# A token gate worked in five batches in place of seven, with its logit matmuls one step later

## The chip, the cores and the metric

One core of one Trainium2 chip. The time is the device time of one execution, in microseconds (us); the profile is of one execution of the same program, and its times count from the start of its span.

## The reference

Three layers in a row, all on 4608 tokens of width 512; the kernel must give the last one's output.

```python
q_c, k_c, v_c = (a.reshape(B, H, S // 64, 64, D) for a in (q, k, v))   # B 8, H 8, S 576, D 64
s = np.matmul(q_c, k_c.transpose(0, 1, 2, 4, 3)) / np.sqrt(D)
p = np.exp(s - s.max(-1, keepdims=True))
x = np.matmul(p / (p.sum(-1, keepdims=True) + 1e-9), v_c)              # then x as [4608, 512]

xn = x / (np.linalg.norm(x, axis=-1, keepdims=True) + 1e-6)
en = expert_emb / (np.linalg.norm(expert_emb, axis=-1, keepdims=True) + 1e-6)
logits = xn @ en.T / tau                                               # 8 experts
idx, gate = logits.argmax(1), softmax(logits).max(1)
x = gate[:, None] * (np.maximum(x @ w1[idx], 0) @ w2[idx])             # one expert a token, F = 1024

h = x @ w_in                                                           # 512 -> 2048
out = (h / (1 + np.exp(-1.702 * h))) @ w_out
```

## The kernel before

The tokens are 36 tiles of 128. The order of the instructions on every engine is the order in which the program writes them; nothing is scheduled behind it. The program has three parts: attention with the gate, the experts, the last layer.

**Attention and gate.** One loop with `n` from 0 to 38 (a step). In step `n` different tiles are at different points:

- TensorE transposes a half of the next q and k (`emit_T`, L307), makes the scores of tile n (`emit_S`, L334), transposes the softmax numerators of tile n-1 (`emit_PT`, L357), multiplies tile n-2 by v (`emit_PV`, L379) and transposes the result of tile n-5 into the layout that the gate needs (`emit_XT`, L431; its second half reads what GpSimd makes). At the end of the step it makes the logits of the same tile n-5 (`emit_L`, L454) in PSUM bank `gb`.
- VectorE takes the row maximum of the scores (`max_S`, L341) and subtracts it (L344), copies the transposed tile out of PSUM (`evac_XT`, L439), scales the result of tile n-3 and rounds it to fp16 (`emit_X`, L405, L410, L415) and divides tile n-2 by its sum (`emit_x`, L387, L389, L391). These are nine instructions a step. From tile 30 on the copy is made by ScalarE (L437); from tile 33 on VectorE makes the rounding rest itself (L420).
- ScalarE copies the transposed q and k (L312, four a step) and the transposed numerators (L364), takes the exponential (L351) and the sum of squares of tile n-3 (`emit_sq`, L399).
- GpSimd makes the rounding rest of tile n-3 (L417, L418; below a pair is called X(t), t being the tile) and issues indirect DMAs.

**The gate** works on a batch of tiles when the last tile of the batch is there: `norm` (the inverse norm of x) is queued by the last tile's `emit_X`, `gate` (argmax, softmax weight, place of each token in its expert's list) by the last tile's `emit_L`. Both are Python generators in one queue `todo`; `drip(1)`, which stands at ten places of a step, issues the next VectorE instruction of the queue's first entry. So a batch's instructions are strewn singly between those of the steps. In the middle of `gate` TensorE counts ranks (L545 to L548, also in bank `gb`); `drip` passes four places before it.

When a batch's places (`pi_all`) are there, one indirect DMA a tile writes token number and weight into a table in HBM (`place`, L494, below a scatter). Even tiles write `mtab[0]`, odd ones `mtab[1]`; a scatter waits until the scatter before it on the same table has landed. `scat()` issues one if any is due: one at the start of a step, and one after X while more than four are left (any are left, from step 30).

Once 24 tiles are gated (`NPART`) the most used expert is chosen, its weights are loaded and split into two fp16 halves (`first_split`; ScalarE L786, VectorE L791, GpSimd L788 and L789) from step 33 on, and three tiles of its tokens are looked up (`find`, L851, two gathers from the tables) and fetched (`fetch`, L858, L864). `turn` transposes a fetched tile by DMA from the SP queue (L872).

**The turn to the experts.** In steps 36 to 38 and behind the loop the first quarter products of expert tiles 0 and 1 (`mm1_part`, L888) stand between the last attention work. Behind the loop the last batch is gated, its scatters are issued, the tables for all expert tiles are worked out (`tables`), and `find(3)`, `fetch(3)`, `turn(3)` bring the first tile that needs every token's place. Then the SP queue loads the next expert's weights. After that come 36 more expert tiles and the last layer, a long run of matmuls.

Of the kernel before, what the change touches and what calls it, by code (L numbers as in the profile page):

```python
# [10 lines left out]
F16 = mybir.dt.float16  # L11
# [4 lines left out]
ALU = mybir.AluOpType  # L16
# [18 lines left out]
def kernel(  # L35
# [13 lines left out]
    nc = tc.nc  # L49
    B, H, S, D = q.shape  # L50
    NT, DM = out.shape
    NE = emb.shape[0]
# [7 lines left out]
    NTILE = NT // 128  # L60
# [15 lines left out]
    att = att_stack.enter_context(tc.tile_pool(name="att", bufs=1))  # L76
# [364 lines left out]

    batches = [(0, 8), (8, 8), (16, 4), (20, 4), (24, 4), (28, 4), (32, 4)]
    DR = [1, 1, 1]
    lg_t = {}

    def emit_L(t):
        bi = [j for j, (a, n) in enumerate(batches) if a <= t < a + n][0]
        t0, n = batches[bi]
        if t == t0:
            o = 0 if bi + 1 < len(batches) else 208  # L450
            lg_t[bi] = gb[:, o:o + 2 * n * NE].rearrange("p (a e) -> p a e", a=n)
        xT = xT_t.pop(t)
        for c in range(2 * KD):
            nc.tensor.matmul(  # L454
                lg_t[bi][:, t - t0, :], xT[:, c, :], enT[:, c % KD, :],
                start=(c == 0), stop=(c == 2 * KD - 1),
            )
# [4 lines left out]
    def small(nm, n, dt=F32, w=None, bufs=1):  # L462
        t = att.tile([128, 8] if w is None else [128, 8, w], dt, tag="g_" + nm, name="g_" + nm, bufs=bufs)
        return t[:, 0:n]
# [3 lines left out]
    def norm(bi):  # L468
        t0, n = batches[bi]
        ssc, y = ss_all[:, t0:t0 + n], rn_all[:, t0:t0 + n]  # L470
        yield from rsqrt(y, small("t", n, I32), small("a", n), ssc)
        nc.vector.tensor_tensor(out=y, in0=y, in1=ssc, op=ALU.mult)
        yield
        nc.vector.tensor_scalar(y, y, 1e-6, None, op0=ALU.add)
        yield
        nc.vector.reciprocal(out=y, in_=y)
        yield
        isx = is_all[:, t0:t0 + n]
        nc.vector.tensor_scalar(
            isx.bitcast(I32), si_all[:, t0:t0 + n], float((BIAS - X_TOP) << 23), None, op0=ALU.add  # L480
        )
        yield
        nc.vector.scalar_tensor_tensor(
            out=y, in0=y, scalar=itau[:, 0:1], in1=isx, op0=ALU.mult, op1=ALU.mult
        )
        yield

    pi_all = att.tile([128, NTILE], I32, name="pi_all")
    scats = deque()
# [10 lines left out]
    def scat():  # L500
        if scats and scats[0][0] < now[0]:
            scats.popleft()[1]()

    def gate(bi):
# [8 lines left out]
        yield  # L513
        nc.vector.tensor_tensor(
            out=l, in0=l, in1=rn_all[:, T].unsqueeze(2).to_broadcast([128, n, NE]), op=ALU.mult
        )
# [16 lines left out]
        yield  # L533
        oh = att.tile([128, 8, NE], F16, tag="g_oh", name="g_oh", bufs=2)[:, 0:n]
        nc.vector.tensor_tensor(
# [5 lines left out]
        yield "pe"  # L541
        rkf = gb[:, 128:128 + n * NE]
        rk = rkf.rearrange("p (a e) -> p a e", a=n)
# [428 lines left out]
    def end_L(t):  # L972
        emit_L(t)
        for bi, (t0, nn) in enumerate(batches):
            if t == t0 + nn - 1:
                todo.append(gate(bi))
# [14 lines left out]
    back = {LATE + 2: LATE - 2}  # L991
    back.update((t + 3, t) for t in range(LATE, NTILE))
    for n in range(NTILE + 3):
        now[0] = n
# [9 lines left out]
        for f in ev[1]:  # L1004
            f()
        turned = []
        if n - 1 in back:
# [15 lines left out]
        issue_v(v_due(n))  # L1023
        if len(scats) > (4 if n < 30 else 0):
            scat()
        on(n, exp_S)
# [3 lines left out]
        if n in back:  # L1030
            emit_XT(back[n])
        for t in sorted(turned):
            end_L(t)
        if n >= NTILE - 5 and fl_n[0] < 8:
# [474 lines left out]
```

## Time and profile before

| what | value |
|---|---|
| time, median of 3 executions | 1449.27 us (1449.14 to 1451.39) |
| time of the profiled execution | 1442.4 us |
| its span in the trace | 1440.7 us |
| attention steps 5 to 31 (first L341 of step 5 to that of step 32) | 39.03 to 193.06 us |
| last L341 (step 35) | 215.14 us |
| last scatter of the last batch | 268.50 us |
| first matmul of expert tile 3 | 283.67 us |

The span begins with the first instruction and ends with the last; the time has some 2 us around it. A step is measured from one L341 of VectorE to the next, there being one in each step up to 35.

### The profile page before, as it was taken

Reading aid. Unit: us, or ns where it says so; the run is one execution under the profiler, and the core shown is the slowest. Engines: PE = TensorE matmul, PEld = TensorE weight load, DVE = VectorE, ACT = ScalarE, POOL = GpSimd, SP = SyncE. Lnnn points to the kernel's source line nnn. Section 1 sums busy time; section 2 is a strip of 40 time slices with the busy share of each in tenths; the row PEclk is TensorE's granted clock in tenths of the full one; section 3 lists DMA queues with packets and bytes.
Section 4 is the critical chain, followed back from the end, with each engine's and each line's share of the span. In section 5 each row is a group of like instructions: output and inputs, shape, how many; then the busy total and the mean of one; then the engine's idle time right before and its main releaser. Section 6 shows DMA issues by size and latency. Waiting matters only on the chain.

```text
span 1440.7 us, 31953 instructions
## 1 busy us (share of the span) xinstructions
PE 1300.4 (90%) x12802; PEld 915.1 (64%) x12802; DVE 855.3 (59%) x1681; ACT 640.1 (44%) x1125; POOL 722.7 (50%) x648
## 2 busy tenths in 40 slices
PE   6777664778989899999989999999999999999998
PEld 4666554556656667767575766758484857566673
DVE  3888886636775667876566372808173644638160
ACT  6986753224453435543453342516152524434250
POOL 1445657535666565564156262717264553626261
PEclk8998976989999999999989999999999999999999
DMA  9887865275775556885310202011020202020000
GB/s 209 216 191 173 167 131 143 68 211 132 209 209 128 162 167 183 255 215 146 69 38 16 45 1 59 2 37 23 23 38 15 45 16 45 9 51 1 30 1 30
DMA packets 196279, 140.71 MB, mean 98 GB/s; under 512 B 129928, under 2 KB 167816, under 8 KB 196112
## 3 DMA queue, kind: packets, MB, share of 16 engines
q1 hardware_dynamic: 183184, 108.39, 32.8%
q0 software_dynamic: 12768, 30.10, 6.2%
q8 instruction: 102, 1.67, 0.5%
q14 instruction: 65, 0.53, 0.1%
q10 hardware_dynamic: 160, 0.02, 0.0%
HBM read 89.00 MB, written 29.80 MB: 82 GB/s over the span
## 4 chain that ended last, share of the span: by engine, by line
PE 50%; DMA 3%; issue 0%; DVE 0%; POOL 0%; ACT 0%; POOLq 0%; DVEq 0%; ACTq 0%
PE pb L1338 6%; PE pd L1338 6%; PE pa L1338 6%; DMA xg<-xs,mt 3%; PE pc L1338 3%; PE gb L1338 3%; PE pa L1453 2%; PE pa L1452 2%; PE pa L1451 2%; PE pd L1451 2%; PE pd L1452 2%; PE pd L1453 2%; PE pb L1452 2%; PE pb L1451 2%; PE pb L1453 2%; PE gb L1452 1%
## 5 line engine op out<-in xcount | busy, mean ns | idle before, releaser
L1338 PEld LDWEIGHTS <-wS 128*128 128x128 f16 x3024 | 297.1, 98 | 42.4 <-issue 5.2
L888 PE MATMUL ph<-xTm,w1HL 128*128 128x128 f16 x3744 | 234.7, 226 | 38.8 <-DMA xTm<-xg 8.1
L888 PEld LDWEIGHTS <-w1HL 128*128 128x128 f16 x3744 | 225.5, 101 | 55.8 <-issue 19.5
L1363 POOL TENSOR_TENSOR w2HL<-z,w1HL 128x512 f16<-128x512 f32 x144 | 217.2, 1524 | 82.8 <-ACT w1HL L1362 81.3
L921 PE MATMUL py<-w2HL,hT 128*128 128x512 f16 x936 | 208.2, 379 | 0.0
L921 PEld LDWEIGHTS <-hT 128*128 128x128 f16 x936 | 89.9, 98 | 101.5
L1458 POOL DMA_INDIRECT out_dram<-y,idc x36 | 35.4, 982 | 235.0 <-ACT y L1457 195.2
L1356 ACT ACTIVATE z<-z 128x512 f32<-128x512 f32 x144 | 88.3, 629 | 107.0 <-DVE z L1353 54.4
L955 POOL DMA_INDIRECT ys<-y,idx_y x39 | 39.1, 1002 | 146.7 <-ACT hT L895 60.1
L1359 DVE TENSOR_TENSOR z<-stgB,z 128x512 f32<-128x512 f32 x108 | 105.3, 1001 | 0.0
L851 POOL DMA_INDIRECT mt<-mtab,idx_g x78 | 88.3, 1132 | 32.9 <-issue 19.7
L1453 PEld LDWEIGHTS <-w2HL 128*128 128x128 f16 x576 | 56.4, 98 | 67.9
L1451 PEld LDWEIGHTS <-w1HL 128*128 128x128 f16 x576 | 56.4, 98 | 67.0
L1452 PEld LDWEIGHTS <-w1HL 128*128 128x128 f16 x576 | 56.4, 98 | 67.0
L1362 ACT ACTIVATE w1HL<-z 128x512 f16<-128x512 f32 x144 | 86.9, 625 | 8.4 <-DVE z L1359 8.4
L417 POOL TENSOR_TENSOR x<-x,sx_all 128x512 f32<-128x512 f32 x33 | 34.3, 1039 | 85.9 <-DVE rd L387 36.8
L896 DVE SCALAR_TENSOR_TENSOR hT<-ph,hT 128x512 f16<-128x512 f32 x78 | 51.0, 683 | 42.8 <-ACT hT L895 40.5
L1175 DVE SCALAR_TENSOR_TENSOR d_f<-raw_o,d_t 128x512 int32<-128x512 int32 x32 | 68.2, 2132 | 3.1
L895 ACT ACTIVATE hT<-ph 128x512 f16<-128x512 f32 x78 | 44.3, 590 | 53.9 <-PE ph L888 49.8
L1384 DVE TENSOR_TENSOR stgB<-stgB,pb 128x512 f32<-128x512 f32 x28 | 19.1, 684 | 81.3 <-PE pb L1338 76.1
L934 ACT ACTIVATE ysq<-py 128x512 f16<-128x512 f32 x39 | 23.1, 593 | 93.8 <-PE py L921 76.2
L1384 DVE TENSOR_TENSOR stgB<-stgB,pd 128x512 f32<-128x512 f32 x27 | 18.5, 684 | 76.4 <-PE pd L1338 76.4
(277 smaller groups left out, 2756.0 us busy)
## 6 DMA issues: line engine op xcount, KB each, us to landing
stg<-in_moe_w_dram SPq DMA_DIRECT2D x14, 1024.0 KB
stgB<-in_moe_w_dram SPq DMA_DIRECT2D x14, 1024.0 KB
vt<-in_v_dram SPq DMA_DIRECT2D x64, 144.0 KB
xs<-xr SPq DMA_DIRECT2D x36, 256.0 KB
raw_o<-in_moe_w_in_dram SPq DMA_DIRECT2D x16, 512.0 KB
raw_o<-in_moe_w_out_dram SPq DMA_DIRECT2D x16, 512.0 KB
ku<-in_k_dram SPq DMA_DIRECT2D x12, 512.0 KB
qu<-in_q_dram SPq DMA_DIRECT2D x12, 512.0 KB
```

The costliest lines, as they stand in the source:

```text
L851: nc.gpsimd.indirect_dma_start(out=mt_t[i][a][:, :], out_offset=None, in_=mtab[a][:, :], in_offset=bass.IndirectOffsetOnAxis(ap=idx_g[:, i ...
L888: nc.tensor.matmul(p[:, f % 4], wt[:, c, fs], xT[:, a, :], start=(c == 0 and a == 0 and wt is w1H), stop=(c == KD - 1 and wt is w1L),)
L921: nc.tensor.matmul(p, hT[:, a, :], wt[:, c, :], start=st, stop=sp)
L1175: nc.vector.scalar_tensor_tensor(out=fi, in0=hi, scalar=-(1 << 31), in1=t, op0=ALU.bitwise_and, op1=ALU.bitwise_or)
L1338: nc.tensor.matmul(dst, wS[a][:, o, kc, fs], rhs(b, kc), start=first and ab == 0 and kc == 0 and n == 0, stop=(kc == 1 and n == 2), skip_g ...
L1356: nc.scalar.activation(out=z, in_=z, func=AF.Sigmoid, scale=1.702 * 2.0 ** -G_EXP)
L1359: nc.vector.tensor_tensor(out=z, in0=c, in1=z, op=ALU.mult)
L1362: nc.scalar.activation(out=dst[0], in_=z, func=AF.Copy)
L1363: nc.gpsimd.tensor_tensor(out=dst[1], in0=z, in1=dst[0], op=ALU.subtract)
L1451: nc.tensor.matmul(p, gT[0][:, h, c, tt], wo[0][:, c, :], start=(c == 0), stop=False)
L1452: nc.tensor.matmul(p, gT[0][:, h, c, tt], wo[1][:, c, :], start=False, stop=False)
L1453: nc.tensor.matmul(p, gT[1][:, h, c, tt], wo[0][:, c, :], start=False, stop=(c == KG - 1))
```

## The change

The seven batches (8, 8, 4, 4, 4, 4, 4 tiles) become five (10, 10, 4, 6, 6). In `norm` the scale of the tile is folded into the addition and the temperature is taken into a multiplication of `gate`. The logits of a tile are made at the start of the step after its copy rather than at the end of the same step, up to step 34. After X up to two scatters may be issued in place of one, and from step 28 on none are held back. Columns of bank `gb` are laid out anew and tiles are made for ten.

```diff
-    batches = [(0, 8), (8, 8), (16, 4), (20, 4), (24, 4), (28, 4), (32, 4)]
+    batches = [(0, 10), (10, 10), (20, 4), (24, 6), (30, 6)]
...
-            o = 0 if bi + 1 < len(batches) else 208
+            o = 0 if bi + 1 < len(batches) else 416
...
-        nc.vector.tensor_scalar(y, y, 1e-6, None, op0=ALU.add)
+        nc.vector.scalar_tensor_tensor(
+            out=y, in0=y, scalar=1e-6, in1=sx_all[:, t0:t0 + n], op0=ALU.add, op1=ALU.mult
+        )
...
-        )
-        yield
-        nc.vector.scalar_tensor_tensor(
-            out=y, in0=y, scalar=itau[:, 0:1], in1=isx, op0=ALU.mult, op1=ALU.mult
         )
...
-        nc.vector.tensor_tensor(
-            out=l, in0=l, in1=rn_all[:, T].unsqueeze(2).to_broadcast([128, n, NE]), op=ALU.mult
+        nc.vector.scalar_tensor_tensor(
+            out=l, in0=l, scalar=itau[:, 0:1], in1=rn_all[:, T].unsqueeze(2).to_broadcast([128, n, NE]),
+            op0=ALU.mult, op1=ALU.mult,
         )
...
-        rkf = gb[:, 128:128 + n * NE]
+        rkf = gb[:, 272:272 + n * NE]
...
+        if n <= NTILE - 2:
+            for t in turned:
+                end_L(t)
         turned = []
...
-        if len(scats) > (4 if n < 30 else 0):
-            scat()
+        for _ in range(2):
+            if len(scats) > (4 if n < 28 else 0):
+                scat()
...
-        for t in sorted(turned):
-            end_L(t)
+        if n >= NTILE - 2:
+            for t in sorted(turned):
+                end_L(t)
```

How the instructions stand now is shown at three places. In the built program a batch has 33 VectorE instructions before the change and 32 after it.

TensorE between step 5 and step 6, where the eight logit matmuls (L454, two rows shown) and the transposes of the next k (L307) meet:

```order
 L379 MATMUL db<-vt_89,PT 64x65 x16
-L454 LDWEIGHTS xTa
-L454 MATMUL gb<-enT,xTa 128x16
...
 L307 MATMUL tp<-identF,ku 128x128 x8
+L454 LDWEIGHTS xTa
+L454 MATMUL gb<-enT,xTa 128x16
...
 L431 LDWEIGHTS xr
```

The logits have moved behind the transposes of q and k and stand directly ahead of `emit_XT`.

GpSimd where the first batch's table entries are scattered (L494 before, L492 now), before the change:

```order
L494 DMA mtab1_77<-meta_154,pi_all_178 36864x2
L494 DMA mtab0_76<-meta_154,pi_all_178 36864x2
L417 TENSOR_TENSOR x_1656<-x_1656,sx_all_173 128x512
L418 TENSOR_TENSOR xr_1718<-x_1656,xr_1718 128x512
```

and now (these are the scatters of tiles 1 to 6 about X(15)):

```order
L492 DMA mtab1_77<-meta_154,pi_all_178 36864x2
L492 DMA mtab0_76<-meta_154,pi_all_178 36864x2
L492 DMA mtab1_77<-meta_154,pi_all_178 36864x2
L417 TENSOR_TENSOR x_1850<-x_1850,sx_all_173 128x512
L418 TENSOR_TENSOR xr_1912<-x_1850,xr_1912 128x512
L492 DMA mtab0_76<-meta_154,pi_all_178 36864x2
L492 DMA mtab1_77<-meta_154,pi_all_178 36864x2
L492 DMA mtab0_76<-meta_154,pi_all_178 36864x2
```

Two scatters between one X and the next became three; there are three in two gaps of the first batch, in three gaps of the second, and in one of the third batch (tiles 20 to 23), behind which all six gathers of `find(0)` to `find(2)` stand in one run ahead of X(30).

VectorE around the scaling of tile 34 (L405) in step 37, before the change:

```order
L509 COPY g_dl_3932<-gb_74 128x32
L512 TENSOR_TENSOR g_l_3934<-gb_74,g_dl_3932 128x32
L514 TENSOR_TENSOR g_l_3934<-g_l_3934,rn_all_177 128x32
L519 TENSOR_REDUCE g_mx_3937<-g_l_3934 128x4
L521 TENSOR_TENSOR g_l_3934<-g_l_3934,g_mx_3937 128x32
L526 SCALAR_TENSOR_TENSOR g_w_3972<-g_l_3934,io_re_128 128x32
L532 TENSOR_REDUCE g_mw_3974<-g_w_3972 128x4
L405 TENSOR_SCALAR si_all_172<-ss_all_171 128x1
```

and now:

```order
L391 TENSOR_TENSOR x_3823<-db_170,rd_3822 128x2x4x64
L576 CAST pi_all_178<-g_pf_3828 128x6
L790 SCALAR_TENSOR_TENSOR w1HL_79<-stg1_82,w1HL_79 128x512
L405 TENSOR_SCALAR si_all_172<-ss_all_171 128x1
```

The seven instructions of the gate of tiles 28 to 31 that stood ahead of it are gone; that batch no longer exists, and the gate of tiles 24 to 29 has ended by then.

## Rows read from the trace of the kernel before

**Rows 1.** The page, first part: busy us, share, instructions of each engine.

```profile
PE 1300.4 (90%) x12802; PEld 915.1 (64%) x12802; DVE 855.3 (59%) x1681; ACT 640.1 (44%) x1125; POOL 722.7 (50%) x648
```

**Rows 2.** Timeline, expert tiles 3 and 4: start, us, work, idle before, releaser.

```profile
283.67 8.02 PE L888 MATMUL ph<-xTm,w1HL 128*128 128x128 f16 x96 [6.60 <-DVE y L951]
...
305.02 5.71 PE L888 MATMUL ph<-xTm,w1HL 128*128 128x128 f16 x62 [8.14 <-DMA xTm<-xg]
```

**Rows 3.** Windows: length, busy PE, PEld, DVE, ACT, POOL (instructions), clock, DMA.

```profile
39.03:61.55 22.52, 17.89 (x461) 15.45 (x461) 18.25 (x45) 21.70 (x42) 10.51 (x11) 1.00 0.89 216
...
39.03:161.86 122.83, 89.78 (x2051) 76.83 (x2050) 104.20 (x300) 96.56 (x184) 63.85 (x60) 0.91 0.84 191
...
161.86:229.83 67.97, 38.08 (x785) 31.57 (x783) 54.13 (x174) 37.27 (x71) 42.28 (x42) 0.75 0.65 131
```

**Rows 4.** Lines of VectorE, 39.03 to 161.86: busy, mean ns, idle before.

```profile
L341 DVE TENSOR_REDUCE mx<-sp 128x8 f32<-128x512 f32 x23 | 15.9, 689 | 15.2 <-PE sp L334 15.2
```

**Rows 5.** Timeline, step 14, the second half of a batch's gate.

```profile
86.04 0.35 PE L454 MATMUL gb<-enT,xTa 128*128 128x16 f16 x8 [2.07 <-DVE g_po L572]
...
89.75 0.69 DVE L341 TENSOR_REDUCE mx<-sp 128x8 f32<-128x512 f32 x1 [2.17 <-PE sp L334]
```

**Rows 6.** Timeline, steps 10 and 17, without gate work.

```profile
61.55 0.69 DVE L341 TENSOR_REDUCE mx<-sp 128x8 f32<-128x512 f32 x1 [0.62 <-PE sp L334]
...
65.60 1.17 POOL L418 TENSOR_TENSOR xr<-x,xr 128x512 f16<-128x512 f32 x1
...
102.27 0.61 PE L431 MATMUL sp<-ident,xr 128*128 128x128 f16 x8
...
103.57 0.69 DVE L341 TENSOR_REDUCE mx<-sp 128x8 f32<-128x512 f32 x1 [0.60 <-PE sp L334]
```

**Rows 7.** Timeline, scatters of tiles 1 and 3, and TensorE behind them.

```profile
95.12 1.01 POOL L494 DMA_INDIRECT mtab<-meta,pi_all  x1 [0.17 <-issue]
...
103.86 1.01 POOL L494 DMA_INDIRECT mtab<-meta,pi_all  x1 [4.16 <-DMA mtab<-meta,pi_all]
...
109.27 0.61 PE L431 MATMUL sp<-ident,xr 128*128 128x128 f16 x4 [2.12 <-POOL xr L418]
```

**Rows 8.** Timeline of GpSimd, scatters of tiles 9, 11 and 13.

```profile
144.02 1.01 POOL L494 DMA_INDIRECT mtab<-meta,pi_all  x1 [0.16 <-issue]
...
150.01 1.01 POOL L494 DMA_INDIRECT mtab<-meta,pi_all  x1 [0.67 <-DMA mtab<-meta,pi_all]
...
154.99 1.01 POOL L494 DMA_INDIRECT mtab<-meta,pi_all  x1 [0.39 <-DMA mtab<-meta,pi_all]
```

**Rows 9.** Timeline, the last batch's first and third scatter.

```profile
262.80 1.34 POOL L494 DMA_INDIRECT mtab<-meta,pi_all  x1 [0.82 <-DVE ttmp L647]
...
266.89 1.31 POOL L494 DMA_INDIRECT mtab<-meta,pi_all  x1 [1.49 <-DMA mtab<-meta,pi_all]
```

**Rows 10.** Timeline of GpSimd, a find, a split and a fetch.

```profile
212.21 0.98 POOL L851 DMA_INDIRECT mt<-mtab,idx_g  x1 [0.15 <-issue]
213.50 1.19 POOL L851 DMA_INDIRECT mt<-mtab,idx_g  x1 [0.30 <-issue]
214.70 1.06 POOL L788 TENSOR_TENSOR stg<-stg,w_pow 128x512 f32<-128x512 f32 x1
...
222.05 0.19 POOL L858 TENSOR_TENSOR mt<-mt,mt 128x2 int32<-128x2 int32 x1
...
223.52 1.05 POOL L788 TENSOR_TENSOR stg<-stg,w_pow 128x512 f32<-128x512 f32 x1
```

**Rows 11.** Timeline, TensorE behind X(32).

```profile
229.89 0.61 PE L431 MATMUL sp<-ident,xr 128*128 128x128 f16 x4 [5.44 <-POOL xr L418]
```

**Rows 12.** Timeline, steps 37 and 38: squares of tiles 34, 35, scaling of 34.

```profile
233.79 0.63 ACT L399 ACTIVATE sq<-x 128x512 f32<-128x512 f32 x1 [0.65 <-DVE is_all L479]
...
239.24 0.14 DVE L405 TENSOR_SCALAR si_all<-ss_all 128x1 int32<-128x1 int32 x1
...
244.75 0.62 ACT L399 ACTIVATE sq<-x 128x512 f32<-128x512 f32 x1
```

More of the change, by code (lines that the diff above doesn't have):

```diff
@@ L462, in small @@
     def small(nm, n, dt=F32, w=None, bufs=1):
-        t = att.tile([128, 8] if w is None else [128, 8, w], dt, tag="g_" + nm, name="g_" + nm, bufs=bufs)
+        t = att.tile([128, 10] if w is None else [128, 10, w], dt, tag="g_" + nm, name="g_" + nm, bufs=bufs)
         return t[:, 0:n]
@@ L533, in gate @@
         yield
-        oh = att.tile([128, 8, NE], F16, tag="g_oh", name="g_oh", bufs=2)[:, 0:n]
+        oh = att.tile([128, 10, NE], F16, tag="g_oh", name="g_oh", bufs=2)[:, 0:n]
         nc.vector.tensor_tensor(
@@ L992 @@
     back.update((t + 3, t) for t in range(LATE, NTILE))
+    turned = []
     for n in range(NTILE + 3):
```

## The prediction

> **What bounds the kernel now.** I read the page first, to see which part has room. TensorE is busy 90% of the span [rows 1]; the experts and the last layer are matmul after matmul and the change does not touch them. So it can only move the moment at which they begin. The timeline shows that moment: the matmuls of expert tile 3 start at 283.67 after 6.60 us of idle TensorE, those of tile 4 at 305.02 after 8.14, the latter for a DMA [rows 2]. By the program the way there is one chain: the last batch's gate, its scatters, `find(3)`, `fetch(3)`, `turn(3)`, and behind `turn(3)` on the SP queue the next weights, in whose traffic tile 4's transfer stands. TensorE is waiting at its end, so what the chain's start gains or loses passes to the end of the kernel in full.
>
> The chain's start is set by attention. The windows, cut where steps begin, show two kinds of step. Steps 5 to 9 hold no gate work: 22.52 us for five, 4.50 each, and ScalarE is busy 21.70 of it [rows 3]. There ScalarE is the bound, and nothing in this change makes it faster. Steps 5 to 26 together take 122.83 us; 22 steps at 4.50 would be 99.1, so the gate costs 23.7 us there. VectorE ran 300 instructions in it [rows 3]; 22 steps at nine are 198 and one more begins at the window's edge, so 101 belong to the gate: 0.235 us of lengthened step for each. That is the price of a gate instruction here, waits included.
>
> Within that price VectorE waited 15.2 us for scores [rows 4]. Of these 0.60 a step is ScalarE's limit showing [rows 6]; the rest has a place. In step 14 the logits waited 2.07 us on TensorE for the gate's product with the ranks (both use `gb`), the transposes and the scores stood behind them, and VectorE then waited 2.17 for the scores [rows 5].
>
> GpSimd is the third thing to read. Its X pair ends 5.2 us after a step's L341 (61.55 to 66.77), and TensorE wants it two steps later, for the second half of `emit_XT`, 1.0 us ahead of that step's L341 (103.57, the transposes having begun at 102.27) [rows 6]: with steps of 4.50 a pair may be 2.8 us late. A scatter waits for the one before it on its table. From one start to the other that took 8.7 us (95.12 to 103.86), and the X behind it made TensorE wait 2.12 [rows 7]; it took 6.0 and 5.0 in a quieter place [rows 8] and 4.1 in the last batch [rows 9]. I call this the landing.
>
> **The change part by part.**
>
> *Fewer gate instructions.* Two batches of 33 go and five lose one each (the order shows one, not two): 71 fewer. Up to step 26 the order has 66 where there were 101. 35 x 0.235 = **8.2 us less**. By busy time the price is nearly the same: 18.25 us of VectorE in five empty steps make 80.3 for 22, and (104.20 - 80.3) / 101 = 0.237. The least is half of that: an empty step leaves VectorE (22.52 - 18.25) / 5 = 0.85 us free, and what is removed from a step with few gate instructions falls into that gap. I take 8.2, since most gate steps hold eight to ten. The longer rows (80 columns for 64) I cost at nothing: a row's length is the small part of instructions this short, and 0.02 us on 32 would be under 1 us.
>
> *Logits behind the transposes of q and k.* TensorE no longer holds these transposes back while it waits for `gb` or for the copy. The steps that gain are those with a batch's second half. Of these two lie in the stretch after the change (16 and 26); three did before, and step 14 shows 2.17 [rows 5]. I take three quarters of it for each: **3.3 less**. It is nothing if scores still come last for another reason, and 6.5 if two thirds of all waits in gate steps (15.2 less 0.6 for each of nine steps without gate work leave 9.8, for three batches) go [rows 4]. In empty steps it gains nothing, ScalarE being full.
>
> *Three scatters between two X's.* Here the change adds a wait, and what is queued behind it on GpSimd is X, and behind X `emit_XT` and the scores on TensorE. With landing L, from the first L341 of step 17, the first batch runs so: X(14) ends at 5.2, scatters start at 5.3 and 6.6, the third at 5.3 + L. With L = 5.5, X(15) ends at 14.1 where TensorE wants it at 12.5: 1.6 late. The next three start at 14.3, 16.3 and 19.8, X(16) ends at 23.0 and is wanted at 17.0 + 1.6: 4.4 late. Together 6.0; the row of before already held 2.1 of such a wait [rows 7], so **3.9 more**. The same walk gives 3.2 in place of 6.0 for L = 4.1, and 12.4 for L = 8.7.
>
> *Steps 27 to X(32).* Before, from 161.86 to 229.83, 67.97 us [rows 3]; TensorE at its end waits 5.44 us for X(32) [rows 11], so GpSimd is the bound. It now holds 14 scatters in place of eight, but the six gathers of the finds stand in one run and do not each wait for a landing. Walked in the same way, with 1.29 for a gather, 2.2 for an X or a split, 1.47 for a fetch [rows 10] and the step lengths above, X(32) ends at 67.2: **0.8 less**. L = 4.1 gives 60.7 (7.3 less), L = 8.7 gives 86.9 (18.9 more).
>
> *Steps 37 and 38.* Tile 34's squares end at 234.4, but its scaling starts at 239.24, behind seven gate instructions; the squares of tile 35 follow at 244.75 [rows 12]. Without them the scaling can follow the split, about 4 us sooner, and TensorE's next quarter with it; VectorE's division of tile 35 and TensorE's earlier work take part of it back. I take **3.0 less**, between 0 and 4.8.
>
> *Six scatters in the last batch in place of four.* The third started 4.1 us after the first [rows 9]; another pair puts the same distance on the chain, with TensorE idle at its end: **4.1 more**. Nothing hides it. `find(3)` comes that much later, `turn(3)` on SP with it, and the weights behind that.
>
> Which L? Rows give 4.1 to 8.7. I take 5.5, between the two of rows 8, which are successive scatters amid gate work, as here; 8.7 lies in a burst of loads, 4.1 where few are left. The sum: -8.2 - 3.3 + 3.9 - 0.8 - 3.0 + 4.1 = **-7.3 us**. The profiled execution took 1442.4 and would take 1435.1; the median of the runs is 6.9 above the profiled one, and I set the sum against it: 1449.3 - 7.3 = **1442.0**.
>
> Against this stands a fixed cost. The Trainium skill, "DMA: Bandwidth & Descriptors", section "Anatomy of one DMA — SWDGE (gpsimd) path", puts a DMA issued from GpSimd at about 2.0 us plus its bytes, whatever else runs. With the 1.0 us of issue in rows 8 that would make the landing an estimated 3.0, the three scatters nearly free and the sum -23 (the first rival's). The rows, 4.1 to 8.7, differ with the traffic and decide it.
>
> **The rivals.**
>
> *Landings are short.* With fewer waits elsewhere scatters may land sooner than any row shows. At L = 3.0, 1.1 below the shortest row, the walks give 1.0 (net -1.1) for the first batch and 56.4 (-11.6) for steps 27 on: -8.2 - 3.3 - 1.1 - 11.6 - 3.0 + 4.1 = -23.1, **1426**. For it: the third scatter of rows 8 waited only 0.39. Against: every landing in the rows is longer.
>
> *GpSimd becomes the bound: slower.* At L = 8.7, +10.3 and +18.9 in place of 3.9 and -0.8: +18.8, **1468**; at 7.0, about +5, **1454**. The sign turns at 6.4. For it: the empty steps 17 to 21, where the first batch's scatters fall, move data at 216 GB/s [rows 3], as in the burst of rows 7. Against: once TensorE stalls, it frees load buffers more slowly and the traffic thins.
>
> *Nothing comes of it.* If the logits' move gives nothing, a gate instruction costs half of what I take, and the rest stands, the sum is -8.2/2 + 3.9 - 0.8 - 3.0 + 4.1 = +0.1, **1449**. That the description promises two operations a batch and the program drops one is worth 5 x 0.235 = 1.2 us and decides nothing.
>
> The transfers are not the next bound: 122.83 us at 191 GB/s are 23.5 MB, which at 216 GB/s take 109 us, 14 less than now [rows 3], more than the terms ask. TensorE's clock is 1.00 in the empty steps and 0.91 over the stretch [rows 3]; a denser TensorE may keep it up, more stalls may drop it, and I cost neither.
>
> **How the numbers follow.** What a measurement of this kernel tells from no change is about 0.2%, 2.9 us. The forecast, L between 4.1 and 6.0, has 0.45 and its own range of 1433 to 1446; short landings 0.18; landings over 6.4 have 0.22; nothing comes of it 0.15. Faster by 0.2%: nearly all of the first two and a little of the last, 0.65. Within: 0.15. Slower: 0.20. The range, 1427 to 1455, leaves out the ends of the two rivals.
>
> **What the profile of the changed kernel would show.** Between the first L341 of step 5 and that of step 27 under 117 us, with 265 VectorE instructions. In steps 16 and 26 a wait before L341 under 1 us, and L454 with hardly any. At X(15) and X(16) L431 waiting for L418, some 6 us together; if that is over 10, or the third scatters wait over 5 us, GpSimd has become the bound and I am wrong. From step 27 to the end of X(32) about 67 us. From the last batch's first scatter to its last about 10 us in place of 5.7, and tile 3's matmuls still waiting. If they no longer wait, the chain is not where I put it, and the gain of attention is not the gain of the kernel.

## The result and the profile after

The changed kernel takes 1456.8 us in the median of 22 runs, the kernel before 1449.2 in 22 runs on the same chip: a ratio of 1.0067, 95% interval 1.0049 to 1.0084. The ratio is taken over the fast executions alone, so it is not quite that of the two medians, 1.0052. The change makes the kernel slower; the forecast was 0.5% faster. The profiled execution took 1449.5 us and its span is 1447.8 us, 7.1 more than before.

The page's first part [rows 1] shows that the work did shrink: 71 VectorE instructions fewer, 12 us of VectorE less. The time did not follow it.

```profile
PE 1308.7 (90%) x12800; PEld 917.1 (63%) x12800; DVE 843.2 (58%) x1610; ACT 637.7 (44%) x1123; POOL 721.7 (50%) x648
```

The end of the chain, on the timeline [rows 2]: expert tile 3 starts at 290.46, 6.8 us later than before. From there to the end of the span it is 1157.3 us, against 1157.0. So all of the loss lies ahead of tile 3.

```profile
290.46 7.25 PE L887 MATMUL ph<-xTm,w1HL 128*128 128x128 f16 x96 [12.27 <-DMA xTm<-xg]
...
308.21 8.35 PE L887 MATMUL ph<-xTm,w1HL 128*128 128x128 f16 x96 [5.32 <-DMA xTm<-xg]
```

The windows, cut as before [rows 3]: steps 5 to 9, steps 5 to 26, and step 27 to the end of X(32) at 232.78.

```profile
38.33:59.33 21.00, 18.67 (x460) 15.33 (x459) 18.24 (x45) 20.63 (x41) 10.14 (x10) 1.00 0.94 225
38.33:158.44 120.11, 91.02 (x2070) 75.03 (x2073) 95.36 (x264) 94.09 (x181) 59.07 (x55) 0.91 0.91 197
158.44:232.78 74.34, 41.70 (x780) 33.02 (x769) 49.56 (x155) 37.75 (x73) 46.74 (x47) 0.70 0.58 121
```

From one stretch to the next: step 5 starts 0.7 us sooner; steps 5 to 26 take 120.1 in place of 122.8; step 27 to X(32) 74.3 in place of 68.0; X(32) to tile 3 57.7 in place of 53.8. Together -0.7 - 2.7 + 6.4 + 3.8 = +6.8. The empty steps take 4.20 us, not 4.50, and still the front gained only 2.7 us. The first batch's scatters show why, on the timelines of GpSimd, TensorE and VectorE [rows 7]:

```profile
98.72 1.01 POOL L492 DMA_INDIRECT mtab<-meta,pi_all  x1 [0.16 <-issue]
100.04 1.13 POOL L492 DMA_INDIRECT mtab<-meta,pi_all  x1 [0.30 <-issue]
109.15 0.97 POOL L492 DMA_INDIRECT mtab<-meta,pi_all  x1 [7.99 <-DMA mtab<-meta,pi_all]
...
111.27 1.15 POOL L418 TENSOR_TENSOR xr<-x,xr 128x512 f16<-128x512 f32 x1
```

```profile
112.48 0.61 PE L431 MATMUL sp<-ident,xr 128*128 128x128 f16 x4 [5.39 <-POOL xr L418]
...
120.59 0.61 PE L431 MATMUL sp<-ident,xr 128*128 128x128 f16 x4 [2.45 <-POOL xr L418]
```

```profile
115.47 0.69 DVE L341 TENSOR_REDUCE mx<-sp 128x8 f32<-128x512 f32 x1 [9.46 <-PE ptp L357]
```

Three scatters stand between two X's. The third shares its table with the first, whose landing took 109.15 - 98.72 = 10.4 us; X(15) stands behind it, TensorE's transposes behind X, the scores behind those, and VectorE waits 9.46 us (its row names the transposes that follow the scores on TensorE): step 19 takes 13.35 us.

The wait costs more than itself. The granted clock of TensorE is 1.00 in steps 5 to 9; from 112.48 to 116.20, behind its wait of 5.39 us, it is 0.50 (1.2 of 2.4 GHz), and the scores take 1.14 us where they took 0.69:

```profile
54.55 0.69 PE L334 MATMUL sp<-kuT,quT 64*64 64x64 f32 x32
...
113.02 1.14 PE L334 MATMUL sp<-kuT,quT 64*64 64x64 f32 x32
```

Over step 27 to X(32) the granted clock is 0.70 where it was 0.75, and nearly the same matmuls keep TensorE busy 41.70 us in place of 38.08. How much of these 3.6 us lies on the chain, no run separates.

The second batch repeats the wait for a landing behind step 27, with 171.36 - 163.91 = 7.5 us [rows 8]. Its row names a store as what ended the wait; with four tables (an experiment below) the same scatter waits 0.30 us, so it is the table it waits for:

```profile
163.91 1.01 POOL L492 DMA_INDIRECT mtab<-meta,pi_all  x1 [0.15 <-issue]
...
171.36 0.97 POOL L492 DMA_INDIRECT mtab<-meta,pi_all  x1 [5.17 <-DMA xs<-xr]
...
205.08 0.97 POOL L492 DMA_INDIRECT mtab<-meta,pi_all  x1 [5.19 <-DMA mtab<-meta,pi_all]
```

The last batch, on GpSimd [rows 9]:

```profile
264.51 1.48 POOL L788 TENSOR_TENSOR w2HL<-stg,w2HL 128x512 f16<-128x512 f32 x1
266.15 1.04 POOL L492 DMA_INDIRECT mtab<-meta,pi_all  x1 [0.16 <-issue]
...
270.20 0.97 POOL L492 DMA_INDIRECT mtab<-meta,pi_all  x1 [1.74 <-DMA mtab<-meta,pi_all]
...
276.64 0.97 POOL L492 DMA_INDIRECT mtab<-meta,pi_all  x1 [1.40 <-DMA mtab<-meta,pi_all]
```

From first to last it takes 10.5 us in place of 5.7, and the first no longer waits for VectorE (0.82 in [rows 9]) but follows GpSimd's splits at once: GpSimd is late there by itself.

### The profile page after: what moved, and what is told of

Read it like the earlier page. It is cut to its first block, busy times and chain, and to the rows that moved or that the text cites. A ratio compares the mean times of both kernels' runs of the same rounds, so it can differ in the third digit from the quotient of the medians.

```text
span 1447.8 us, 31872 instructions
## 1 busy us (share of the span) xinstructions
PE 1308.7 (90%) x12800; PEld 917.1 (63%) x12800; DVE 843.2 (58%) x1610; ACT 637.7 (44%) x1123; POOL 721.7 (50%) x648
## 4 chain that ended last, share of the span: by engine, by line
PE 49%; DMA 3%; issue 1%; POOL 0%; ACT 0%; POOLq 0%; DVE 0%; DVEq 0%; ACTq 0%
PE pb L1343 6%; PE pd L1343 6%; PE pa L1343 6%; DMA xg<-xs,mt 3%; PE pc L1343 3%; PE gb L1343 3%; PE pa L1458 2%; PE pa L1457 2%; PE pa L1456 2%; PE pd L1458 2%; PE pd L1456 2%; PE pd L1457 2%; PE pb L1458 2%; PE pb L1456 2%; PE pb L1457 2%; PE gb L1458 1%
## 5 line engine op out<-in xcount | busy, mean ns | idle before, releaser
L1361 ACT ACTIVATE z<-z 128x512 f32<-128x512 f32 x144 | 88.3, 629 | 107.5 <-DVE z L1358 54.7
L1458 PEld LDWEIGHTS <-w2HL 128*128 128x128 f16 x576 | 56.3, 98 | 68.0
L1457 PEld LDWEIGHTS <-w1HL 128*128 128x128 f16 x576 | 56.3, 98 | 67.1
L1456 PEld LDWEIGHTS <-w1HL 128*128 128x128 f16 x576 | 56.3, 98 | 67.0
L1367 ACT ACTIVATE w1HL<-z 128x512 f16<-128x512 f32 x144 | 86.9, 624 | 8.4 <-DVE z L1364 8.4
```

The costliest lines, as they stand in the source:

```text
L1361: nc.scalar.activation(out=z, in_=z, func=AF.Sigmoid, scale=1.702 * 2.0 ** -G_EXP)
L1367: nc.scalar.activation(out=dst[0], in_=z, func=AF.Copy)
L1456: nc.tensor.matmul(p, gT[0][:, h, c, tt], wo[0][:, c, :], start=(c == 0), stop=False)
L1457: nc.tensor.matmul(p, gT[0][:, h, c, tt], wo[1][:, c, :], start=False, stop=False)
L1458: nc.tensor.matmul(p, gT[1][:, h, c, tt], wo[0][:, c, :], start=False, stop=(c == KG - 1))
```

## The experiments

Each kernel was timed in turn with the kernel before on one chip; a ratio is to that kernel. Chips differ (the kernel before takes 1434.7 to 1435.1 us in the first twelve runs' medians, 1445.4 in the last two), so ratios are compared and not times. The stretches of a kernel come from one profiled execution; the executions of one kernel on one chip lie 3 to 24 us apart, so a difference of a us or two between two kernels' stretches is a hint and no proof. The theories: **S**, three scatters between X's wait for landings; **T**, the last batch of six is the loss; **D**, the steps wait for loads; later **N**, the second batch of ten puts its scatters behind step 27, and **Q**, X being late holds the SP queue (the store of x waits in it for X), whose loads then come late. The stretches below are read from the timelines in the same way as above: first L341 of step 5 to that of step 27; from there to the end of X(32); from there to tile 3.

| kernel (batches; scatters after X) | ratio, 95% interval | steps 5 to 26, us | to X(32), us | to tile 3, us |
|---|---|---|---|---|
| before (8,8,4,4,4,4,4; one) | 1 | 122.8 | 68.0 | 53.8 |
| changed (10,10,4,6,6; two) | 1.0067 (1.0049 to 1.0084) | 120.1 | 74.3 | 57.7 |
| changed, one scatter to step 27 | 1.0059 (1.0035 to 1.0082) | 120.5 | 78.0 | 56.3 |
| changed, 10,10,4,4,4,4 | 1.0068 (1.0048 to 1.0088) | 120.8 | 73.7 | 54.4 |
| before, logits moved | 0.9967 (0.9950 to 0.9984) | 117.3 | 65.5 | 56.0 |
| before, two scatters | 1.0052 (1.0032 to 1.0071) | 130.5 | 63.3 | 54.7 |
| changed, four tables | 1.0166 (1.0144 to 1.0188) | 113.4 | 71.3 | 56.2 |
| changed, store later | 1.0008 (0.9997 to 1.0019) | 118.9 | 70.8 | 57.8 |
| changed, 8,8,4,4,6,6; one | 0.9977 (0.9960 to 0.9994) | 117.7 | 64.4 | 55.0 |
| changed, 10,10,4,4,4,4; one to 27 | 1.0074 (1.0056 to 1.0092) | 117.7 | 80.1 | 54.4 |
| 8,8,4,4,6,6; one; store later | 0.9931 (0.9910 to 0.9952) | 112.3 | 62.5 | 55.6 |
| before, store later | 0.9982 (0.9967 to 0.9997) | 121.5 | 64.8 | 54.7 |
| 10,6,4,4,6,6; one | 0.9960 (0.9942 to 0.9978) | 118.9 | 64.6 | 55.4 |
| 8,8,4,4,6,6; two | 1.0052 (1.0033 to 1.0070) | 123.2 | 66.9 | 58.2 |
| 10,6,4,4,6,6; one; store later | 0.9889 (0.9859 to 0.9918) | 115.3 | 61.4 | 54.0 |
| 10,10,4,6,6; one to 27; store later | 0.9979 (0.9950 to 1.0007) | 112.0 | 75.0 | 58.5 |

### One scatter after X

```diff
-        for _ in range(2):
-            if len(scats) > (4 if n < 28 else 0):
+        for _ in range(1 if n < 28 else 2):
+            if len(scats) > (4 if n < 30 else 0):
                 scat()
```

> The changed kernel, but up to step 27 only one scatter may follow X as before the change (four are held back to step 29); two from step 28 on. Theory S (three scatters between two X's wait on GpSimd for landings of 7 to 10 us, and X, the transposes of x and the scores stand behind them): the 9.5 us of idle time in step 19 go, steps 5 to 26 fall from 120.1 us to 108 to 113, and the kernel from 1457 to 1445 to 1450. Rival T (the last batch of six decides the end): steps 5 to 26 get shorter too, but the last batch's scatters still take 10 us on the chain and tile 3 comes at about its 290 us or a little sooner; 1453 to 1457. Rival D (the steps now wait for loads, the DMA share is 0.97 in steps 5 to 16 where it was 0.83): the wait moves from the scatters to q, k, v loads, steps 5 to 26 take 117 us or more and the time stays at 1456.

Steps 19 to 21 fall from 27.5 us to 23.5, but steps 23 and 24 grow (TensorE waits 3.8 us for k there), and the stretch behind step 27 grows to 78.0. Theory S in this form falls: with batches of ten, taking the third scatter out of the gaps gains nothing. The wait moved, as D said it would: up to step 26 TensorE waits 3.2 us for X in place of 9.1, and 12.2 us for loads of k and v in place of 3.4. The last run below, which differs from this one by the store alone, shows why the loads were late.

### The old tail

```diff
-    batches = [(0, 10), (10, 10), (20, 4), (24, 6), (30, 6)]
+    batches = [(0, 10), (10, 10), (20, 4), (24, 4), (28, 4), (32, 4)]
```

> The changed kernel with the old batches at the end (10, 10, 4, 4, 4, 4 tiles), so that the last batch has four tiles again and the gate of tiles 28 to 31 is back ahead of the scaling of tile 34. Theory S: steps 5 to 26 stay at 120 us, the idle time in step 19 stays, and of the 6.8 us by which tile 3 came later only the tail's part (4.8 us between first and last scatter, 3.3 us in the queue ahead of them) can go, less the 3 us that the seven gate instructions take back: 1450 to 1454. Rival T: the tail is the whole loss, and with the old tail the earlier end of step 26 (3.4 us) shows as a gain: 1444 to 1448. Rival D says nothing of the tail: 1456.

The tail returns to 54.4 us and tile 3 starts at 287.81 in the profiled execution, 2.7 us sooner, but over all executions the ratio stays at 1.0068. T falls: the last batch of six is not what makes the kernel slower.

### The logits alone, in the kernel before

```diff
+        if n <= NTILE - 2:
+            for t in turned:
+                end_L(t)
         turned = []
...
-        for t in sorted(turned):
-            end_L(t)
+        if n >= NTILE - 2:
+            for t in sorted(turned):
+                end_L(t)
```

> The kernel before with the logits move alone: the logits of a tile stand at the start of the next step, behind the transposes of q and k, up to step 34. By the recorded prediction this gains 3.3 us in steps with a batch's second half and nothing in empty steps: steps 5 to 9 stay at 4.50 us each; 1446. By the trace of the changed kernel (its empty steps took 4.20) an empty step gains 0.3 us, and with some 13 such steps before step 27 the stretch from 5 to 27 falls by 5 to 8 us from 122.8, the kernel to 1442 to 1445. Rival D: the loads hold the steps, and the time stays at 1449.

Faster by 0.33%, 4.7 us. Empty steps take 4.20. The prediction had them at 4.50 because ScalarE was busy 21.70 of 22.52 us. The timeline shows what the other 0.8 us was: before the change, from step 8 on, ScalarE waits some 0.20 us behind the exponential (L351) for the transposes of k or q, which TensorE holds back behind the logits, and loses the overlap with the next instruction too. Kernel before, ScalarE and TensorE:

```profile
59.19 0.62 ACT L351 ACTIVATE P<-P 128x512 f32<-128x512 f32 x1
60.01 1.29 ACT L312 ACTIVATE kuT<-tp 64x512 f32<-64x512 f32 x2 [0.20 <-PE tp L307]
...
59.11 0.36 PE L454 MATMUL gb<-enT,xTa 128*128 128x16 f16 x8 [0.93 <-DVE si_all L405]
```

The changed kernel at the same place:

```profile
53.79 0.62 ACT L351 ACTIVATE P<-P 128x512 f32<-128x512 f32 x1
54.31 1.28 ACT L312 ACTIVATE quT<-tp 64x512 f32<-64x512 f32 x2
...
53.81 0.35 PE L454 MATMUL gb<-enT,xTa 128*128 128x16 f16 x8
```

0.82 us from start to start has become 0.52: that is the 0.30 of each step. What set the 4.50 was a ring of two other engines: L341, the copy (L439), the logits that wait 0.93 us for VectorE, the transposes, the scores and the next L341. In steps 5 and 6 of the kernel before, ScalarE does not wait (0.52 from start to start) and the steps take 4.51 all the same; ScalarE's wait is that ring reaching it. With the logits moved the ring is open, their row shows no wait, and 4.20 is ScalarE's own pace (busy 20.63 of 21.00 us). An engine busy 96% of a stretch was not yet the bound.

### The two scatters alone, in the kernel before

```diff
-        if len(scats) > (4 if n < 30 else 0):
-            scat()
+        for _ in range(2):
+            if len(scats) > (4 if n < 28 else 0):
+                scat()
```

> The kernel before with the scatter loop alone: up to two scatters after X, none held back from step 28 on; batches of 8, 8, 4, 4, 4, 4, 4 as before. Theory S: the wait of X behind a third scatter is there without any other part of the change, GpSimd's third scatters wait 4 to 8 us in the first two batches, TensorE's wait for the rounding rest of x grows from 11.8 us to over 16 us, and the kernel takes 1453 to 1459. Rivals T and D: the loop costs nothing by itself, 1448 to 1451. The recorded prediction's walk with a landing of 5.5 us gives 1 to 4 us more, 1450 to 1453.

Slower by 0.52%, 7.5 us. Steps 5 to 26 take 7.7 us more; the third scatters of the first two batches wait 6.12 and 4.97 us (both rows name a load of v as what ended the wait; that it is the table, the next run speaks for). TensorE's wait for X grows from 11.8 us to 15.8, just under what was expected; SP's wait for X grows from 38.2 to 45.1 us up to step 26. With batches of eight, S holds.

### Four tables

```diff
-    mtab = [dr.tile([NE * NT, 2], F32, name=f"mtab{a}") for a in range(2)]
+    mtab = [dr.tile([NE * NT, 2], F32, name=f"mtab{a}") for a in range(4)]
...
-            out=mtab[t % 2][:, :],
+            out=mtab[t % 4][:, :],
```

(`find` gathers from four tables and `fetch` adds the four.)

> The changed kernel with four tables in place of two: a scatter shares its table with the fourth before it, so three in a row never wait for one another; each find has four gathers (two more, 1.3 us each on GpSimd) and each fetch two more additions. Theory S (landing waits on GpSimd): the waits of scatters for a landing, 35.8 us between 40 and 330 in the changed kernel, fall under 12; X(15) is no longer 8 us late, step 19 falls from 13.35 us to under 7; the six more gathers of the first three finds take back 7 to 8 us ahead of X(30); 0.998 to 1.003 of the kernel before. Rival D (the loads hold the steps anyway): the scatters' waits go, the steps stay long behind q, k and v loads, 1.005 or more. A third outcome, that a scatter waits for the one before it on the queue and not on its table, would leave the 35.8 us where they are.

The waits of scatters for landings between 40 and 330 fall from 35.8 us to 7.8, step 19 to 7.03, steps 5 to 26 to 113.4: it is the table that a scatter waits for, not the queue. Behind step 27 GpSimd is busy 54.67 us in place of 46.74 for the gathers added, and the stretch takes 3.0 less all the same. Tile 3 starts at 281.98, 8.5 us sooner than in the changed kernel. That the ratio is still far over what S expected comes from behind tile 3, in the experts: from 330 to 600 the gathers keep GpSimd busy 206.5 us in place of 164.5, and TensorE is busy 235.3 in place of 247.6.

### The store of x one step later on SP

```diff
-        nc.sync.dma_start(out=xs[t * 128:(t + 1) * 128, :], in_=xrf)
+        def store():
+            nc.sync.dma_start(out=xs[t * 128:(t + 1) * 128, :], in_=xrf)
+        if t < 30:
+            late.append(store)
+        else:
+            store()
...
+        held, late[:] = list(late), []
         on(n - 3, end_X)
...
         issue_v(v_due(n))
+        for f in held:
+            f()
```

> The changed kernel with the store of a tile's x to HBM one step later in the SP queue, up to tile 29, so that the loads of v, k and q no longer stand behind a store that waits for X. Theory Q (late X holds the SP queue, the loads behind it are issued late, and TensorE later waits for k): SP's wait for X, 25.6 us between 100 and 160, falls under 5, TensorE's waits for ku go, step 27 starts 3 to 6 us sooner and the kernel is 0.2 to 0.5% faster than the changed one: 1.002 to 1.005 of the kernel before. Theory S alone: SP's wait goes too, but X(15) and X(16) are as late as they were and thicker traffic makes the landings longer: 1.006 to 1.010. Rival D: 1.006, no change.

1.0008 where the changed kernel has 1.0067: 0.6%, more than was expected. TensorE's waits for k and v loads in steps 5 to 35 are gone (6.1 us in the changed kernel); SP still waits 18.2 us for X between 95 and 160, not under 5, but with its loads ahead of it. X's own waits stay: step 19 takes 12.35.

### Front and tail apart

```diff
-    batches = [(0, 10), (10, 10), (20, 4), (24, 6), (30, 6)]
+    batches = [(0, 8), (8, 8), (16, 4), (20, 4), (24, 6), (30, 6)]
...
-        for _ in range(2):
-            if len(scats) > (4 if n < 28 else 0):
-                scat()
+        if len(scats) > (4 if n < 30 else 0):
+            scat()
```

> The changed kernel with its front batches and its scatter loop undone: 8, 8, 4, 4, 6, 6 tiles and one scatter after X. Against the kernel with the logits move alone (0.9967 of before) it has one gate operation fewer in each batch and the merged tail. Theory N (batches of ten push the second batch's scatters into the stretch behind step 27, where GpSimd is the bound): steps 5 to 26 take 115 to 118 us, X(32) ends near 222, and only the tail of six costs 2 to 6 us: 0.997 to 1.001. By the recorded terms (3.0 less in steps 37 and 38, 4.1 more in the last batch) 0.9975. Rival T (the tail is the whole loss): 1.002 to 1.005.

0.9977, by its interval not to be told from the logits alone (0.9967): merged tail and shorter `norm` together show no gain. The other half has the batches 10, 10, 4, 4, 4, 4 and the scatter loop of the first experiment:

> The changed kernel with batches of 10, 10, 4, 4, 4, 4 and one scatter after X up to step 27, two from step 28: the front's batches of ten without the three scatters in a gap and without the last batch of six. Theory N: 14 scatters still lie between step 27 and X(32), that stretch takes 73 to 78 us as in the three other kernels with batches of ten, 1.003 to 1.006. Theory S in its first form (three scatters in a gap): with one after X the loss goes, 0.996 to 1.000. Rival T: with the old tail the loss goes too, 0.996 to 1.000.

1.0074, and 80.1 us behind step 27, both over what N expected. The front of tens without three scatters and without the tail has the whole loss. Its windows, and those of the kernel with eights, in steps 5 to 26 and to X(32):

```profile
37.59:155.28 117.69, 90.26 (x2070) 75.26 (x2074) 95.02 (x265) 94.39 (x181) 59.16 (x55) 0.93 0.96 204
155.28:235.40 80.12, 39.84 (x779) 31.95 (x768) 52.71 (x172) 37.82 (x73) 46.73 (x46) 0.70 0.54 111
```

```profile
37.64:155.31 117.67, 88.98 (x2071) 74.36 (x2074) 100.53 (x296) 94.22 (x182) 63.05 (x59) 0.94 0.93 204
155.31:219.70 64.39, 36.61 (x779) 29.02 (x769) 51.01 (x158) 37.99 (x73) 42.77 (x43) 0.74 0.66 137
```

31 VectorE instructions fewer up to step 26 show no gain, and the stretch behind it grows by 15.7 us.

### The store later with eights, and in the kernel before

> Batches of 8, 8, 4, 4, 6, 6 and one scatter after X, the rest as changed (0.9977 of before in its own run), and the store of x one step later on SP. Theory Q as an independent gain (loads behind a store that waits for X come late in every version): TensorE's waits for k and v loads in steps 5 to 35 (11 us without the move) fall under 4, 0.990 to 0.994 of the kernel before. If the move only repairs what the late X of the batches of ten costs: 0.996 to 0.999.

0.9931. Steps 5 to 26 take 112.3 in place of 117.7, TensorE no longer waits for k or v loads.

> The kernel before with the store of x one step later on SP and nothing else. Theory Q as an independent gain: 0.993 to 0.998 of the kernel before. If the move only repairs the late X of the changed kernel, no change: 0.999 to 1.001.

0.9982, just beyond the 0.998 of Q's range: a gain, but a smaller one. Q is an independent gain, in whole or in part; whether it is larger once the logits no longer hold the steps, the intervals don't settle.

### Ten and six; eights with two scatters

Both are the kernel with 8, 8, 4, 4, 6, 6 and one scatter with one edit: the batches (0, 10), (10, 6) in place of (0, 8), (8, 8), or the loop of two scatters.

> As the kernel with 8, 8, 4, 4, 6, 6 and one scatter after X, but the first two batches have 10 and 6 tiles: the first batch is the changed kernel's, the second ends at tile 15 as before the change, so that no more scatters than before fall behind step 27. Theory N (the loss lies in the stretch behind step 27, where ten scatters of a late second batch stand ahead of X): 5 to 26 take 116 to 120 us, step 27 to X(32) 63 to 67, 0.996 to 0.999 of the kernel before. Rival F (the burst of the first ten scatters, with steps 19 and 20 of 10 to 13 us, is the loss): 1.002 to 1.006.

0.9960, and 64.6 us behind step 27. The first batch of ten costs nothing; it is the second of ten, which ends at tile 19, not 15. Between step 27 and X(32) GpSimd issues 14 scatters in every kernel with two batches of ten, 10 here and in the kernels with eights and a merged tail, 9 in the kernel before. N holds, F falls.

> The changed kernel with its front batches alone undone (8, 8, 4, 4, 6, 6), with up to two scatters after X. Theory S (a third scatter in a gap costs by itself, as it did in the kernel before, 1.0052): steps 5 to 26 take 122 to 126 us in place of 117.7, 1.001 to 1.005 of the kernel before. Theory N alone (only the late second batch costs, the loop is free once the logits have moved): 0.996 to 0.999.

1.0052. The loop costs 0.75% by itself with eights, and 5.5 us up to step 26; SP's wait for X up to step 26 is 39.1 us in place of 24.0.

### Both with the store later

> Batches of 10, 6, 4, 4, 6, 6, one scatter after X and the store of x one step later on SP. If the two effects found so far add (0.9960 for the batches, 0.0046 less for the store with batches of eight), 0.991 to 0.993 of the kernel before, the same as the eights with the store later. If the burst of ten scatters costs once the loads are early, 0.995 or more. Steps 5 to 26 between 110 and 115 us, step 27 to X(32) between 61 and 65.

0.9889: 1.1% faster than the kernel before, and faster than the two effects added. Steps 5 to 26 take 115.3 us, at the edge of what was expected. Whether it beats the eights with the store later (0.9931, on another chip) stays open; the intervals touch.

> Batches of 10, 10, 4, 6, 6, one scatter after X up to step 27 (two from 28), and the store of x one step later on SP. Up to step 26 it has 32 gate instructions fewer than the eights with the store later, which took 112.3 us there. If the recorded price of 0.235 us for a gate instruction holds once the loads no longer wait for X, steps 5 to 26 take 104 to 108 us; if loads and landings set these steps (theory D), 111 to 115 and the instructions are worth nothing. Theory N: step 27 to X(32) takes 72 to 80 us all the same, the kernel 0.998 to 1.003 of before; if only SP's wait made that stretch long, 62 to 66 and 0.990 to 0.994.

Steps 5 to 26 take 111.99 us with 264 VectorE instructions, where the eights took 112.34 with 296: 32 gate instructions fewer show no gain here. Against the first experiment, which differs by the store alone, steps 5 to 26 fall from 120.5 us to 112.0, TensorE no longer waits for k or v loads (12.2 us there), and the ratio falls from 1.0059 to 0.9979: the late loads of D were late through Q. Behind step 27 it is still 75.0 us. The timelines of GpSimd and TensorE there:

```profile
189.69 0.98 POOL L499 DMA_INDIRECT mtab<-meta,pi_all  x1 [2.02 <-DMA mtab<-meta,pi_all]
196.77 0.97 POOL L499 DMA_INDIRECT mtab<-meta,pi_all  x1 [6.10 <-DMA mtab<-meta,pi_all]
...
203.84 0.99 POOL L857 DMA_INDIRECT mt<-mtab,idx_g  x1 [2.64 <-DMA mtab<-meta,pi_all]
205.13 0.96 POOL L857 DMA_INDIRECT mt<-mtab,idx_g  x1 [0.30 <-DVE rd L389]
206.40 0.95 POOL L857 DMA_INDIRECT mt<-mtab,idx_g  x1 [0.30 <-issue]
207.65 0.95 POOL L857 DMA_INDIRECT mt<-mtab,idx_g  x1 [0.30 <-issue]
208.62 1.06 POOL L419 TENSOR_TENSOR x<-x,sx_all 128x512 f32<-128x512 f32 x1
```

```profile
200.10 0.61 PE L438 MATMUL sp<-ident,xr 128*128 128x128 f16 x4 [8.90 <-POOL xr L420]
...
210.96 0.61 PE L438 MATMUL sp<-ident,xr 128*128 128x128 f16 x4 [6.23 <-POOL xr L420]
```

TensorE waits 24.3 us for X in this stretch, against 8.4 with eights and the store later. Scatters of a late second batch, then the third batch's, then gathers in a row stand ahead of X, and X is what TensorE wants.

## Why the prediction was wrong, step by step

Two steps failed. Fewer gate instructions were to give 8.2 us and gave about none; the stretch from step 27 to X(32) was to lose 0.8 us and grew by 6.4, its landings being longer than the 5.5 us taken.

**By stretches.** Tile 3's start passes to the end in full: that step was right. The forecast was -7.6 up to step 26 (measured -2.7), -0.8 to X(32) (+6.4), and +1.1 behind it (+3.8).

**Fewer gate instructions, -8.2: the step that failed in the front.** The price of 0.235 us put the whole lengthening of 23.7 us on 101 instructions. But 8.5 of it lay in steps 18 to 20 before the change (22.0 us where three empty ones take 13.5), which hold 17 of these instructions and also the stall of the first scatters. When the gate's instructions leave those steps, the stall stays: in the changed kernel steps 19 to 21 hold none and take 27.5 us. Without such a stall the price is smaller: steps 12, 13, 15 and 16 of the last run hold 31 instructions and take 21.5 us, four empty ones 16.8, so 0.15 each. Two pairs of kernels that up to step 26 differ by two batches of ten in place of eights show what fewer instructions gave: 31 fewer 0.0 us, 32 fewer 0.35 us in steps 5 to 26. In the last run steps 18 to 21 hold none of them and take 24.8 us; with eights and the store later they hold 24 and take 26.6. Loads and landings set these steps. The agreement with the price by busy time was no second proof: both divide by the same count, and busy time does not say what waits.

**Logits, -3.3: right in sign, too small, and for the wrong steps.** Alone it is worth 4.7 us of the kernel and 5.5 up to step 26. That ScalarE is the bound in empty steps, and that they therefore gain nothing, was false, by the 0.30 us shown above. The product with the ranks still holds the logits 1.08 us in step 16 (2.07 in [rows 5]), but VectorE no longer waits for the scores behind it, as forecast.

**Three scatters between X's, +3.9 at a landing of 5.5 us: mis-sized, since no one landing fits.** The first took 10.4 us, the next that was waited for, behind X(15), 4.6 (112.58 to 117.19), and the one after it 10.8 (113.89 to 124.68; its row names VectorE). X(15) and X(16) made TensorE wait 5.39 + 2.45 = 7.8 us, and X(17) 1.30 more, where 6 were forecast; the third scatter waited 7.99, over the 5 at which the forecast would have GpSimd the bound. By itself the loop costs 5.5 us up to step 26 with eights and 7.7 in the kernel before.

**Step 27 to X(32), -0.8: the landing again, and it decided the sign.** 74.3 us, where the walk had 67.2. The landings that GpSimd waited for there took 7.5, 5.1, 9.3, 9.2 and 7.5 us, 7.7 in the mean, where 5.5 was taken. So the second rival, GpSimd becoming the bound, is what came; it was given 0.22. Its walk has 86.9 at a landing of 8.7 and 67.2 at 5.5: by it 7.7 would give some 81, and 74.3 belongs to 6.7. That this lies just over 6.4, where its sum turns, is luck as much as proof. It also counted eight scatters before, where the timeline has nine, and put the clock at nothing. What spoke against it, that stalled TensorE thins the traffic, came in part: while TensorE waited for X(15), from 109.15 to 112.50, the DMA engines moved 15 GB/s, and the landing behind it took 4.6 us; but over steps 5 to 26 the DMA share rose from 0.84 to 0.91. The experiments add where the loss comes from: the second batch's end at tile 19.

**Steps 37 and 38, -3.0: right in size, off the path.** The squares of tile 35 follow X(32)'s end by 11.8 us (244.62) where it was 14.9. But the last batch's first scatter follows X(32) by 33.4 us, before by 33.0: GpSimd, with the scatters of tiles 24 to 29 waiting ahead of three splits, took the place of the chain. In the kernel of eights with one scatter after X and the merged tail it passes on: 30.9 us.

**Two more scatters in the last batch, +4.1: right.** 4.8 measured. Behind the last scatter the way to tile 3 is 1.4 us shorter than before, which the forecast did not have.

**What the prediction didn't name: SP.** The store of x waits on SP for X, and loads of v, k and q stand behind it. From step 5 to X(32) the store waited 98.0 us, before 80.1 (of these 82.9 and 54.2 where the row names X, L418). Putting the store behind the loads gives back 0.6% in the changed kernel. The share of this in the loss itself isn't settled, since the same move gains in all five pairs of kernels that differ by it: 0.18% in the kernel before, 0.46% with eights, 0.7% with ten and six, 0.8% with tens and one scatter.

**What doesn't add up.** With eights the loop costs 0.75%; with tens the ratios show no cost. The stretches give a part of a reason: with tens the loop drains the second batch sooner (74 us behind step 27 in place of 78 to 80). In front it takes 3.1 us with the old tail and nothing with the merged one. This is argued from single executions and not shown by a run of its own.

## What to carry to other kernels

A lengthening divided by the number of instructions is a price only if nothing else lengthens the same steps: look first for the steps that are long, and at who waits there. Larger batches make bursts: what follows each batch (here scatters on a queue that also feeds TensorE) should be walked to the point where it ends, and the batches cut so that this point lies where the queue has room: here ten and six in place of ten and ten. A store that waits for late work, put ahead of loads in one queue, delays the loads: put it behind them.

## What the runs showed of the hardware

A scatter of 128 rows of 8 bytes, 1 KB, takes from start to the start of the next on its table 4.05 us where the DMA engines are nearly idle (266.15 to 270.20) and 10.4 where loads fill them (98.72 to 109.15). The DMA view of the changed kernel, from 98.7 to 109.2 and then from 266 to 270.2 (q1's last figure is the time its packets took, as a share of the 16 engines' span; here it passes 100%):

```profile
DMA packets 3218, 1.52 MB, mean 145 GB/s; under 512 B 1204, under 2 KB 3088, under 8 KB 3216
...
q1 hardware_dynamic: 3152, 1.49, 110.8%
```

```profile
DMA packets 63, 0.02 MB, mean 4 GB/s; under 512 B 62, under 2 KB 62, under 8 KB 62
```

That traffic makes the landing long is read from such pairs of stretches, not shown by a run of its own. The Trainium skill, "DMA: Bandwidth & Descriptors", section "Anatomy of one DMA — SWDGE (gpsimd) path", has a fixed cost of about 2.0 us; with the issue that was an estimated 3.0. No landing that was waited for in these runs was as short; the shortest is 3.63 us (273.01 to 276.64 in the changed kernel).
